# One attention decode kernel: V loads on a second DMA queue, and an output projection in four PSUM banks

## Chip, cores and metric

The kernel runs on one core of one Trainium2 chip. The metric is device time in microseconds for one execution of the whole kernel; each version is given by the median of its runs. The profile is one further look at a single execution, with its own time.

## The reference

One decode step of grouped-query attention with a sliding window, 32 sequences, 32 query heads on 8 key/value heads of 128 elements, bf16. Of the 2048 cached positions only the last W = 512 take part.

```python
B, Sq, D = x.shape                      # 32, 1, 512
Hq, Dh = 32, 128
Hkv, Sk = k_cache.shape[1], k_cache.shape[2]     # 8, 2048
W = min(4096, max(256, Sk // 4))        # 512
rep = Hq // Hkv                         # 4
q = (x @ wq).reshape(B, Sq, Hq, Dh)     # heads moved ahead
k = repeat(k_cache[:, :, Sk - W:, :], rep)
v = repeat(v_cache[:, :, Sk - W:, :], rep)
p = softmax(einsum("bhqd,bhkd->bhqk", q, k) * Dh ** -0.5)
o = einsum("bhqk,bhkd->bhqd", p, v)
return o.reshape(B, Sq, Hq * Dh) @ wo   # (32, 1, 512)
```

Each sequence needs 1 MiB of K and 1 MiB of V. With wq and wo (4 MiB each) that is 72 MiB read from HBM for an output of 32 KB.

## The kernel before

The five engines run their own programs, joined by semaphores. A "batch" is one sequence; its K (and its V) comes as two loads of 512 KB, one per half of the key/value heads (`h` = 0, 1), each into 128 partitions with 4 KB rows. `K_sb` holds `NK` = 6 batches, `V_sb` holds `NV` = 8.

**SP** issues nearly all loads on one DMA queue, in the order of its program: wq in four parts (part 0 at L110, ahead of the block, parts 1 to 3 at L122), then for each `b` `load_k(b)` (L128) and, from `b` = `LEAD` = 5 on, `load_v(b - 5)` (L136). So V follows K at a distance of five batches in the same queue, and after `load_k(31)` come `load_v(26)` to `load_v(31)`. `load_k(b)` waits until PE has transposed batch `b - 6`, `load_v(b)` until PE has done the PV product of batch `b - 8`. Then SP loads wo (L148) into the SBUF space of wq, in four parts cut at heads 0, 10, 20, 28 and 32 (`WO_CUT`), and at the end stores the output (L153). The load of x is issued by ACT ahead of the block (L109).

**PE** computes q transposed (L207) and then runs a loop over `it`. Iteration `it` transposes K of batch `it` (L229, four groups of eight), makes the scores of batch `it - 1` (L246; eight matmuls of 512 columns, four of them beside each other in column groups of 32), and the PV product of batch `it - 6` (L279). The scores of four batches (a "quad") fill one tile `S_ps`, so the softmax runs once per quad; its probabilities are transposed by PE in iterations with `it % 4 == 1` (L261). After the last batch comes the output projection: for each of the 32 heads, four matmuls with 128 columns of wo each, in the four column groups (L301). All 128 add up in one bank, so that the four groups hold four column ranges of the finished output, and `pe_fin` tells that they are done.

**DVE** copies three of the four K^T groups from PSUM (L324), takes the maxima of a quad (L330, L332), scales the probabilities into `P_ex` (L346), copies the PV result into `oT_sb` (L353) and at the end the output (L368).

**ACT** loads its exp table, copies half of q (L375), and then per iteration copies the fourth K^T group (`kt_evac`, L383), per quad computes the exp (`do_exp`, L391) and copies the transposed probabilities (`pt_evac`, L401).

**POOL** makes the constants (`ident`, `perm`, zeros) and copies q into the block layout `QBD` (L189).

The order of instructions within an engine is the order in its program. An engine that waits for a semaphore holds everything behind that wait.

Of the kernel before, what the change touches and what calls it, by code (L numbers as in the profile page):

```python
# [5 lines left out]
BF16 = mybir.dt.bfloat16  # L6
F32 = mybir.dt.float32
ACTF = mybir.ActivationFunctionType
ALU = mybir.AluOpType
# [3 lines left out]
def bass_standalone__sliding_block_cached__sampling_kernel(  # L13
# [8 lines left out]
    B, Sq, D = x.shape  # L22
    _, HKV, SK, DH = k_cache.shape
    HD = wq.shape[1]
    HQ = HD // DH
# [7 lines left out]
    DKT = D // 128  # L33
    SCALE = float(DH) ** -0.5
    P = 128

    NK = 6
    NV = 8
    NKT = 3
    NQB = 8  # L40
    LEAD = 5
    PVLAG = 6
    NQUAD = B // 4
    WO_CUT = (0, 10, 20, 28, 32)

    with ExitStack() as es:
        sb = lambda name, shape, dt: es.enter_context(nc.sbuf_tensor(name, shape, dt))
        ps = lambda name, shape, dt: es.enter_context(nc.psum_tensor(name, shape, dt))
        sem = lambda name: es.enter_context(nc.semaphore(name))

        w_sb = sb("w_sb", [P, DKT * HD], BF16)
        wq_sb = w_sb[:, :].rearrange("p (kt n) -> p kt n", kt=DKT)
        wo_sb = w_sb[:, :].rearrange("p (h n) -> p h n", h=HQ)
# [9 lines left out]
        xT_sb = sb("xT_sb", [P, DKT, 32], BF16)  # L63
        ident = sb("ident", [P, P], BF16)
        perm = sb("perm", [P, G4, NS], BF16)
        x_sb = sb("x_sb", [32, D], BF16)
        out_sb = sb("out_sb", [P, 128], BF16)
        maxv = sb("maxv", [P, NQUAD], F32)
        negmax = sb("negmax", [P, NQUAD], F32)
        sums = sb("sums", [P, NQUAD], F32)  # L70
# [17 lines left out]
        pe_S = sem("pe_S")  # L88
        pe_PT = sem("pe_PT")
        pe_PV = sem("pe_PV")  # L90
        pe_fin = sem("pe_fin")
        pool_perm = sem("pool_perm")
        pool_ex = sem("pool_ex")
        dve_xT = sem("dve_xT")
# [7 lines left out]
        dve_oT = sem("dve_oT")  # L102
        act_exp = sem("act_exp")
        act_PT = sem("act_PT")
        dve_out = sem("dve_out")
        act_warm = sem("act_warm")
        pool_init = sem("pool_init")
        pool_qbd = sem("pool_qbd")
        nc.scalar.dma_start(x_sb[:, :], x.rearrange("b s d -> b (s d)")).then_inc(sem_x, 16)  # L109
        nc.sync.dma_start(wq_sb[:, 0, :], wq[0:P, :]).then_inc(sem_wq[0], 16)  # L110
        block = es.enter_context(nc.Block())

        def score_row(h, j):
# [2 lines left out]
        def cache_rows(cache, b, h):  # L116
            return cache[b, 4 * h:4 * h + 4, SK - W:, :].rearrange("g (s r) d -> s g (r d)", s=NS)

        @block.sync
        def _(sp):  # L120
            for kt in range(1, DKT):
                sp.dma_start(wq_sb[:, kt, :], wq[kt * P:(kt + 1) * P, :]).then_inc(sem_wq[kt], 16)  # L122

            def load_k(b):
                if b >= NK:
                    sp.wait_ge(pe_T[3], b - NK + 1)
                for h in range(2):
                    sp.dma_start(  # L128
                        K_sb[:, b % NK, h].rearrange("p r d -> p (r d)"), cache_rows(k_cache, b, h)
                    ).then_inc(sem_k[b % NK][h], 16)  # L130

            def load_v(b):
                if b >= NV:
                    sp.wait_ge(pe_PV, b - NV + 1)
                for h in range(2):
                    sp.dma_start(  # L136
                        V_sb[:, b % NV, h].rearrange("p r d -> p (r d)"), cache_rows(v_cache, b, h)
                    ).then_inc(sem_v[b % NV], 16)

            for b in range(B + LEAD):  # L140
                if b < B:
                    load_k(b)
                if b >= LEAD:
                    load_v(b - LEAD)
            sp.wait_ge(pe_qt, 1)
            for c in range(4):
                h0, h1 = WO_CUT[c], WO_CUT[c + 1]
                sp.dma_start(  # L148
                    wo_sb[:, h0:h1, :],
                    wo[h0 * DH:h1 * DH, :].rearrange("(h d) n -> d h n", d=P),  # L150
                ).then_inc(sem_wo[c], 16)
            sp.wait_ge(dve_out, 1)
            sp.dma_start(  # L153
                out.rearrange("b s (c n) -> c (b s) n", c=4), out_sb[:, :]
            ).then_inc(sem_out, 16)
            sp.wait_ge(sem_out, 16)

        @block.gpsimd
        def _(pool):
            pool.memset(ident[:, :], 0.0).then_inc(pool_init, 1)  # L160
            pool.wait_ge(pool_init, 1)
            pool.affine_select(
                out=ident[:, :], in_=ident[:, :], compare_op=ALU.not_equal, fill=1.0,
                base=0, pattern=[[-1, P]], channel_multiplier=1,
            ).then_inc(pool_init, 1)
            pool.memset(perm[:, :, :], 0.0).then_inc(pool_perm, 1)
            pool.wait_ge(pool_perm, 1)
            pool.affine_select(
                out=perm[:, :, :], in_=perm[:, :, :], compare_op=ALU.not_equal, fill=1.0,
                base=0, pattern=[[-1, G4], [-G4, NS]], channel_multiplier=1,  # L170
            ).then_inc(pool_perm, 1)
            pool.memset(junk[:, :], 0.0).then_inc(pool_init, 1)
            pool.memset(QBD[:, :, :, :], 0.0).then_inc(pool_init, 1)
            pool.memset(P_ex[:, :, :, :], 0.0).then_inc(pool_ex, 1)
            pool.wait_ge(pool_init, 4)
            pool.wait_ge(dve_qt, 1)
            pool.wait_ge(act_qt, 1)
            for b in range(B):
                if b >= NQB:
                    pool.wait_ge(pe_S, b - NQB + 1)  # L180
                dst = bass.AP(
                    tensor=QBD, offset=(b % NQB) * G * 32 + score_row(0, b % 4),
                    ap=[[NQB * G * 32, P], [G4 * 32 + 16, 2], [32, G4], [1, REP]],
                )
                src = bass.AP(
                    tensor=QT_sb, offset=b,
                    ap=[[HQ * B, P], [G4 * REP * B, 2], [REP * B, G4], [B, REP]],
                )
                pool.tensor_copy(dst, src).then_inc(pool_qbd, 1)  # L189

        @block.tensor
        def _(pe):
# [102 lines left out]
                    pt_transposes((it - 5) // 4)  # L295
            pe.wait_ge(dve_oT, B)
            for hq in range(HQ):
                if hq in WO_CUT:
                    pe.wait_ge(sem_wo[WO_CUT.index(hq)], 16)
                for c in range(4):  # L300
                    ins = pe.matmul(  # L301
                        KT_ps[:, 0, :].bitcast(F32)[32 * c:32 * (c + 1), 0:128],
                        lhsT=oT_sb[:, :, hq],
                        rhs=wo_sb[:, hq, c * 128:(c + 1) * 128],
                        start=(hq == 0), stop=(hq == HQ - 1), tile_position=(0, 32 * c),
                    )
            ins.then_inc(pe_fin, 1)

        @block.vector
        def _(dve):  # L310
# [54 lines left out]
                if it % 4 == 0 and 4 <= it <= B:  # L365
                    softmax_a((it - 4) // 4)
            dve.wait_ge(pe_fin, 1)
            dve.tensor_copy(out_sb[:, :], KT_ps[:, 0, :].bitcast(F32)[:, 0:128]).then_inc(dve_out, 1)  # L368

        @block.scalar  # L370
        def _(act):
            act.wait_ge(pool_init, 3)
            act.activation(junk[:, 1:2], junk[:, 0:1], ACTF.Exp).then_inc(act_warm, 1)
            act.wait_ge(pe_qt, 1)
            act.activation(  # L375
                QT_sb[:, 16:32, :].rearrange("p h b -> p (h b)"), PT_ps[:, 1, :].bitcast(F32), ACTF.Copy
            ).then_inc(act_qt, 1)

            def kt_evac(b):
                if b >= NKT:  # L380
                    act.wait_ge(pe_S, b - NKT + 1)
                act.wait_ge(pe_T[3], b + 1)
                act.activation(  # L383
                    KT_sb[:, b % NKT, 1, 8:16, :, :], KT_ps[:, 3, :], ACTF.Copy
                ).then_inc(act_T, 1)

            def do_exp(q):
                act.wait_ge(dve_sm, 2 * q + 2)
                if q >= 1:
                    act.wait_ge(dve_P, 4 * q)  # L390
                act.activation(  # L391
                    P_f32[:, :], S_ps[:, :], ACTF.Exp,
                    bias=negmax[:, q:q + 1], scale=SCALE, accum_out=sums[:, q:q + 1],
                ).then_inc(act_exp, 1)

            def pt_evac(q):
                if q >= 2:
                    act.wait_ge(pe_PV, 4 * (q - 2) + 4)
                for i in range(2):
                    act.wait_ge(pe_PT, 2 * q + i + 1)  # L400
                    act.activation(  # L401
                        PT_sb[:, q % 2, 8 * i:8 * i + 8, :].rearrange("p r n -> p (r n)"),
                        PT_ps[:, i, :], ACTF.Copy,
                    ).then_inc(act_PT, 1)

            for it in range(B + 2):
                if it < B:
                    kt_evac(it)
                if it % 4 == 0 and 4 <= it:
                    do_exp((it - 4) // 4)  # L410
                if it % 4 == 1 and 5 <= it:
                    pt_evac((it - 5) // 4)


# [26 lines left out]
```

## Time and profile before

| what | value |
|---|---|
| median of 3 runs | 198.01 us (197.91 to 198.32) |
| the profiled execution | 198.32 us, span 196.5 us, 6073 instructions |
| PE busy | 142.8 us (73%) |
| DVE busy | 99.8 us (51%) |
| ACT busy | 56.5 us (29%) |
| POOL busy | 12.1 us (6%) |
| mean TensorE clock granted | 0.851 of full |
| moved by DMA | 75.95 MB, mean 386 GB/s |

The span goes from the first to the last instruction; the execution's own time is longer by what lies around it, here 1.8 us. Busy time counts neither waiting nor the issue of a DMA. Names such as SPq and ACTq stand for an engine's sequencer while it issues a DMA; the transfer itself is run by 16 DMA engines afterwards. In a list of instructions in order of time each line gives the start, the duration, the engine, the source line, the operation with its output and input tiles, how many instructions are merged, and in brackets the idle time of the engine before it with what ended it. In a table by windows each line gives the stretch, its length, the busy time of PE, PE's weight loads, DVE, ACT and POOL with their counts, the granted clock, the busy share of the DMA engines and GB/s.

### The profile page before, as it was taken

To read this page: it belongs to the slowest core of one execution; us is meant where nothing else is said; L and a number is where in the kernel's file an instruction comes from. 1 tells how busy PE (TensorE), PEld (TensorE's weight loads), DVE (VectorE), ACT (ScalarE), POOL (GpSimd) and SP (SyncE) were. 2 spreads that over 40 slices of the span, in tenths; PEclk is the share of its full clock that TensorE was granted. 3 is DMA by queue.
4 is the path that set the end of the run, shared out by engine and by line. 5 is a ranking of instruction groups with operands and counts; after the bars stand their busy time and mean duration, and the time that the engine had idled before them with its cause. 6 is when DMAs were issued, how large, how long until landed. Compare 5 with 4: busy or idle time off the path is not lost.

```text
span 196.5 us, 6073 instructions
## 1 busy us (share of the span) xinstructions
PE 142.8 (73%) x2692; PEld 116.4 (59%) x2692; DVE 99.8 (51%) x187; ACT 56.5 (29%) x67; POOL 12.1 (6%) x43
## 2 busy tenths in 40 slices
PE   0448994987787797749786979779997599746423
PEld 0337773875575576637665858656975477535322
DVE  0006789645774479424952695457645647541000
ACT  3002434433262145203342325232432052320000
POOL 8102000000000010000000000000000000000000
PEclk9999999699999799985999797996699759955555
DMA  5999999999999999999999999999999999999970
GB/s 205 425 417 409 411 405 409 411 409 405 409 409 405 408 407 409 410 407 410 404 409 408 409 409 404 410 406 409 406 408 408 408 409 403 409 404 350 338 253 16
DMA packets 23374, 75.95 MB, mean 386 GB/s; under 512 B 2325, under 2 KB 6453, under 8 KB 22837
## 3 DMA queue, kind: packets, MB, share of 16 engines
q1 hardware_dynamic: 23300, 75.54, 97.5%
q8 instruction: 21, 0.34, 0.7%
q10 hardware_dynamic: 48, 0.03, 0.2%
q14 instruction: 5, 0.03, 0.0%
HBM read 75.53 MB, written 0.03 MB: 384 GB/s over the span
## 4 chain that ended last, share of the span: by engine, by line
SPq 52%; DMA 37%; PE 7%; issue 2%; DVE 0%
DMA K_sb<-in_k_cache_dram 32%; SPq L136 25%; SPq L128 18%; SPq L148 8%; DMA w_sb<-in_wo_dram 5%; PE KT_ps L229 4%; PE QO_ps L279 1%; PE S_ps L246 1%; SPq L122 1%; PE KT_ps L301 0%; SPq L110 0%; DVE out_sb L368 0%
## 5 line engine op out<-in xcount | busy, mean ns | idle before, releaser
L229 PE MATMUL KT_ps<-perm,K_sb 128*128 128x128 bf16 x1024 | 76.0, 238 | 20.7 <-DMA K_sb<-in_k_cache_dram 20.5
L324 DVE COPY KT_sb<-KT_ps 128x1024 bf16<-128x1024 bf16 x96 | 63.3, 687 | 54.0 <-PE KT_ps L229 53.7
L229 PEld LDWEIGHTS KT_ps<-perm,K_sb 128*128 128x128 bf16 x1024 | 67.5, 108 | 27.1 <-DMA K_sb<-in_k_cache_dram 26.0
L383 ACT ACTIVATE KT_sb<-KT_ps 128x1024 bf16<-128x1024 bf16 x32 | 32.7, 1023 | 81.8 <-PE KT_ps L229 81.8
L279 PEld LDWEIGHTS QO_ps<-PT_sb,V_sb 128*128 128x128 bf16 x1024 | 28.2, 98 | 17.4 <-issue 12.7
L279 PE MATMUL QO_ps<-PT_sb,V_sb 128*128 128x16 bf16 x1024 | 31.1, 171 | 3.7 <-DMA V_sb<-in_v_cache_dram 1.9
L346 DVE TENSOR_SCALAR P_ex<-P_f,recip 32x512 bf16<-32x512 f32 x32 | 25.3, 792 | 1.1
L246 PE MATMUL S_ps<-KT_sb,QBD 128*32 128x512 bf16 x256 | 21.4, 414 | 0.0
L401 ACT ACTIVATE PT_sb<-PT_ps 128x1024 bf16<-128x1024 bf16 x16 | 15.5, 1020 | 20.4 <-PE PT_ps L261 20.4
L261 PE MATMUL PT_ps<-ident,P_ex 128*128 128x128 bf16 x128 | 11.8, 266 | 9.6 <-DVE P_ex L346 9.6
L261 PEld LDWEIGHTS PT_ps<-ident,P_ex 128*128 128x128 bf16 x128 | 10.1, 122 | 10.7 <-DVE P_ex L346 10.7
L189 POOL COPY QBD<-QT_sb 128x32 bf16<-128x32 bf16 x32 | 7.4, 245 | 117.9 <-PE S_ps L246 108.0
L353 DVE CAST oT_sb<-QO_ps 128x32 bf16<-128x32 f32 x32 | 5.9, 183 | 8.9 <-PE QO_ps L279 8.8
L301 PE MATMUL KT_ps<-w_sb,oT_sb 128*32 128x128 bf16 x128 | 4.3, 313 | 6.6 <-DMA w_sb<-in_wo_dram 6.6
L207 PE MATMUL PT_ps<-xT_sb,w_sb 128*128 128x32 bf16 x128 | 4.1, 188 | 6.2 <-DMA w_sb<-in_wq_dram 6.2
L301 PEld LDWEIGHTS KT_ps<-w_sb,oT_sb 128*32 128x32 bf16 x128 | 3.3, 158 | 7.4 <-DMA w_sb<-in_wo_dram 4.7
L207 PEld LDWEIGHTS PT_ps<-xT_sb,w_sb 128*128 128x128 bf16 x128 | 3.7, 104 | 6.6 <-DMA w_sb<-in_wq_dram 4.6
L330 DVE TENSOR_REDUCE maxv<-S_ps 128x1 f32<-128x512 f32 x8 | 5.5, 691 | 4.0 <-PE S_ps L246 4.0
L391 ACT ACTIVATE P_f<-S_ps,negmax 128x512 f32<-128x512 f32 x8 | 5.5, 687 | 5.4 <-DVE negmax L332 5.4
L246 PEld LDWEIGHTS S_ps<-KT_sb,QBD 128*32 128x32 bf16 x256 | 3.9, 96 | 3.7 <-issue 1.0
L316 DVE CAST QT_sb<-PT_ps 128x512 bf16<-128x512 f32 x1 | 0.7, 691 | 10.0 <-PE PT_ps L207 10.0
L368 DVE CAST out_sb<-KT_ps 128x128 bf16<-128x128 f32 x1 | 0.3, 292 | 10.7 <-PE KT_ps L301 10.7
(20 smaller groups left out, 11.9 us busy)
## 6 DMA issues: line engine op xcount, KB each, us to landing
K_sb<-in_k_cache_dram SPq DMA_DIRECT2D x64, 512.0 KB, 15.6
V_sb<-in_v_cache_dram SPq DMA_DIRECT2D x64, 512.0 KB, 15.4
w_sb<-in_wq_dram SPq DMA_DIRECT2D x4, 1024.0 KB, 8.4
w_sb<-in_wo_dram SPq DMA_DIRECT2D x2, 1280.0 KB, 19.3
w_sb<-in_wo_dram SPq DMA_DIRECT2D x1, 1024.0 KB, 12.7
w_sb<-in_wo_dram SPq DMA_DIRECT2D x1, 512.0 KB, 9.9
x_sb<-in_x_dram ACTq DMA_DIRECT2D x1, 32.0 KB, 3.2
out_dram<-out_sb SPq DMA_DIRECT2D x1, 32.0 KB
```

Of the source, the lines that this page charges most:

```text
L128: sp.dma_start(K_sb[:, b % NK, h].rearrange("p r d -> p (r d)"), cache_rows(k_cache, b, h)).then_inc(sem_k[b % NK][h], 16)
L136: sp.dma_start(V_sb[:, b % NV, h].rearrange("p r d -> p (r d)"), cache_rows(v_cache, b, h)).then_inc(sem_v[b % NV], 16)
L148: sp.dma_start(wo_sb[:, h0:h1, :], wo[h0 * DH:h1 * DH, :].rearrange("(h d) n -> d h n", d=P),).then_inc(sem_wo[c], 16)
L207: ins = pe.matmul(PT_ps[:, h // 16, :].bitcast(F32)[:, (h % 16) * 32:(h % 16 + 1) * 32], lhsT=wq_sb[:, kt, h * DH:(h + 1) * DH], rhs=xT_sb ...
L229: ins = pe.matmul(KT_ps[:, t, i * 128:(i + 1) * 128], lhsT=K_sb[:, b % NK, h, 8 * (t % 2) + i, :], rhs=perm[:, :, :], start=True, stop=Tru ...
L246: ins = pe.matmul(S_ps[32 * c:32 * c + 32, :], lhsT=QBD[:, b % NQB, g, :], rhs=KT_sb[:, b % NKT, h, :, c, :], start=(j == 0 and h == 0), s ...
L261: ins = pe.matmul(PT_ps[:, r // 8, (r % 8) * 128:(r % 8 + 1) * 128], lhsT=P_ex[:, r, :, :].rearrange("p s g -> p (s g)"), rhs=ident[:, :], ...
L279: ins = pe.matmul(QO_ps[:, 16 * h:16 * h + 16], lhsT=V_sb[:, b % NV, h, r, :], rhs=PT_sb[:, q % 2, r, :].rearrange("p (c n) -> p c n", c=G ...
L324: dve.tensor_copy(KT_sb[:, b % NKT, t // 2, 8 * (t % 2):8 * (t % 2) + 8, :, :], KT_ps[:, t, :]).then_inc(dve_T, 1)
L346: dve.tensor_scalar(P_ex[rows, :, :, c], P_f32[rows, :].rearrange("p (r s) -> p r s", r=NR), recip[rows, q:q + 1], None, op0=ALU.mult,).th ...
L383: act.activation(KT_sb[:, b % NKT, 1, 8:16, :, :], KT_ps[:, 3, :], ACTF.Copy).then_inc(act_T, 1)
L401: act.activation(PT_sb[:, q % 2, 8 * i:8 * i + 8, :].rearrange("p r n -> p (r n)"), PT_ps[:, i, :], ACTF.Copy,).then_inc(act_PT, 1)
```

## The change

All V loads move from SP to ACT. ACT issues `load_v(0)` ahead of its loop and `load_v(it + 1)` at the top of iteration `it`, before `kt_evac(it)`; the wait for the PV product of eight batches earlier moves along. SP keeps x, wq, K, wo and the output. The load of x is now the first on SP's queue, inside the block, and wq part 0 comes behind it. SP loads wo after a new semaphore `act_v`, which ACT raises in iteration 31, one iteration after it has issued the last V load. wo comes in four parts of eight heads.

The output projection has one matmul of 512 columns per head instead of four of 128. Head `hq` goes to column group `hq % 4` and to bank `hq % 4`, so that four banks hold partial sums over eight heads each. DVE copies two of the partial sums into `X_sb` and ACT two; a further matmul with `R_sb` (four identity blocks of 32 below each other, made by POOL) adds the four; ACT copies the sum to `out_sb`, now 32 rows of 512, and SP stores it.

```diff
-    WO_CUT = (0, 10, 20, 28, 32)
+        X_sb = sb("X_sb", [P, D], BF16)
+        R_sb = sb("R_sb", [P, 32], BF16)
-        out_sb = sb("out_sb", [P, 128], BF16)
+        out_sb = sb("out_sb", [32, D], BF16)
...
-        nc.scalar.dma_start(x_sb[:, :], x.rearrange("b s d -> b (s d)")).then_inc(sem_x, 16)
-        nc.sync.dma_start(wq_sb[:, 0, :], wq[0:P, :]).then_inc(sem_wq[0], 16)
...
         def _(sp):
-            for kt in range(1, DKT):
+            sp.dma_start(x_sb[:, :], x.rearrange("b s d -> b (s d)")).then_inc(sem_x, 16)
+            for kt in range(DKT):
                 sp.dma_start(wq_sb[:, kt, :], wq[kt * P:(kt + 1) * P, :]).then_inc(sem_wq[kt], 16)
...
-            for b in range(B + LEAD):
-                if b < B:
-                    load_k(b)
-                if b >= LEAD:
-                    load_v(b - LEAD)
+            for b in range(B):
+                load_k(b)
             sp.wait_ge(pe_qt, 1)
+            sp.wait_ge(act_v, 1)
             for c in range(4):
-                h0, h1 = WO_CUT[c], WO_CUT[c + 1]
                 sp.dma_start(
-                    wo_sb[:, h0:h1, :],
-                    wo[h0 * DH:h1 * DH, :].rearrange("(h d) n -> d h n", d=P),
+                    wo_sb[:, c * 8:(c + 1) * 8, :],
+                    wo[c * 1024:(c + 1) * 1024, :].rearrange("(h d) n -> d h n", d=P),
                 ).then_inc(sem_wo[c], 16)
-            sp.wait_ge(dve_out, 1)
-            sp.dma_start(
-                out.rearrange("b s (c n) -> c (b s) n", c=4), out_sb[:, :]
-            ).then_inc(sem_out, 16)
+            sp.wait_ge(act_out, 1)
+            sp.dma_start(out.rearrange("b s d -> b (s d)"), out_sb[:, :]).then_inc(sem_out, 16)
...
         def _(pool):
...
+            pool.wait_ge(pool_init, 2)
+            pool.tensor_tensor(R_sb[:, :], ident[:, 0:32], ident[:, 32:64], ALU.add).then_inc(pool_R, 1)
...
         def _(pe):
...
             for hq in range(HQ):
-                if hq in WO_CUT:
-                    pe.wait_ge(sem_wo[WO_CUT.index(hq)], 16)
-                for c in range(4):
-                    ins = pe.matmul(
-                        KT_ps[:, 0, :].bitcast(F32)[32 * c:32 * (c + 1), 0:128],
-                        lhsT=oT_sb[:, :, hq],
-                        rhs=wo_sb[:, hq, c * 128:(c + 1) * 128],
-                        start=(hq == 0), stop=(hq == HQ - 1), tile_position=(0, 32 * c),
-                    )
+                c = hq % 4
+                if hq % 8 == 0:
+                    pe.wait_ge(sem_wo[hq // 8], 16)
+                ins = pe.matmul(
+                    KT_ps[:, c, :].bitcast(F32)[32 * c:32 * (c + 1), :],
+                    lhsT=oT_sb[:, :, hq],
+                    rhs=wo_sb[:, hq, :],
+                    start=(hq < 4), stop=(hq >= HQ - 4), tile_position=(0, 32 * c),
+                )
             ins.then_inc(pe_fin, 1)
+            pe.wait_ge(pool_R, 3)
+            pe.wait_ge(dve_x, 2)
+            pe.wait_ge(act_x, 2)
+            pe.matmul(
+                QO_ps[0:32, :], lhsT=R_sb[:, :], rhs=X_sb[:, :], start=True, stop=True, tile_position=(0, 0),
+            ).then_inc(pe_out, 1)
...
         def _(dve):
...
             dve.wait_ge(pe_fin, 1)
-            dve.tensor_copy(out_sb[:, :], KT_ps[:, 0, :].bitcast(F32)[:, 0:128]).then_inc(dve_out, 1)
+            for c in range(2):
+                dve.tensor_copy(
+                    X_sb[32 * c:32 * (c + 1), :], KT_ps[:, c, :].bitcast(F32)[32 * c:32 * (c + 1), :]
+                ).then_inc(dve_x, 1)
...
         def _(act):
...
+            def load_v(b):
+                if b >= NV:
+                    act.wait_ge(pe_PV, b - NV + 1)
+                for h in range(2):
+                    act.dma_start(
+                        V_sb[:, b % NV, h].rearrange("p r d -> p (r d)"), cache_rows(v_cache, b, h)
+                    ).then_inc(sem_v[b % NV], 16)
+
+            load_v(0)
             for it in range(B + 2):
+                if it + 1 < B:
+                    load_v(it + 1)
+                if it == B - 1:
+                    act.activation(junk[:, 0:1], junk[:, 1:2], ACTF.Copy).then_inc(act_v, 1)
                 if it < B:
                     kt_evac(it)
...
+            act.wait_ge(pe_fin, 1)
+            for c in range(2, 4):
+                act.activation(
+                    X_sb[32 * c:32 * (c + 1), :], KT_ps[:, c, :].bitcast(F32)[32 * c:32 * (c + 1), :], ACTF.Copy
+                ).then_inc(act_x, 1)
+            act.wait_ge(pe_out, 1)
+            act.activation(out_sb[:, :], QO_ps[0:32, :], ACTF.Copy).then_inc(act_out, 1)
```

## The prediction

> **What bounds the kernel now.** I read the 40 slices of the span first, then the queues, the chain that ended last, and the instructions of the last 32 us in order of time.
>
> ```profile
> DMA  5999999999999999999999999999999999999970
> GB/s 205 425 417 409 411 405 409 411 409 405 409 409 405 408 407 409 410 407 410 404 409 408 409 409 404 410 406 409 406 408 408 408 409 403 409 404 350 338 253 16
> q1 hardware_dynamic: 23300, 75.54, 97.5%
> SPq 52%; DMA 37%; PE 7%; issue 2%; DVE 0%
> ```
>
> The 16 DMA engines are full from the second slice to the last but one, at about 409 GB/s, all from one queue. The chain is queue and DMA: no compute engine bounds the stream. So an edit costs time if it starts the stream later, leaves a hole in it, slows it, or leaves more work behind its end. The end is this, from the last score-key transposes on:
>
> ```profile
> 165.94 0.90 PEld L229 LDWEIGHTS KT_ps<-perm,K_sb 128*128 128x128 bf16 x16 [0.38 <-DMA K_sb<-in_k_cache_dram]
> ...
> 181.72 1.00 PE L279 MATMUL QO_ps<-PT_sb,V_sb 128*128 128x16 bf16 x32 [0.67 <-DMA V_sb<-in_v_cache_dram]
> 182.76 0.19 DVE L353 CAST oT_sb<-QO_ps 128x32 bf16<-128x32 f32 x1 [1.48 <-PE QO_ps L279]
> ...
> 192.95 0.65 PE L301 MATMUL KT_ps<-w_sb,oT_sb 128*32 128x128 bf16 x16 [0.25 <-DMA w_sb<-in_wo_dram]
> 193.66 0.29 DVE L368 CAST out_sb<-KT_ps 128x128 bf16<-128x128 f32 x1 [10.70 <-PE KT_ps L301]
> 193.97 0.69 SPq L153 DMA_DIRECT2D out_dram<-out_sb  x1
> ```
>
> The second half of K31 lands at 165.94. Six V batches follow it in the one queue (load_k(31) is followed by load_v(26) to load_v(31)); V31 lands at 181.72, so 15.78 us for 6 MiB, **2.63 us per MiB**. The wo weights land 11.23 us later, at 192.95. From K31 to the last oT copy (182.95) the compute chain takes 17.01 us; 0.38 of it is extra waiting for V31 (0.67 against the 0.29 that the matmul group before it waits), so it needs **16.63 us**. Today this chain is hidden: 10 us of wo loads come after it, and three of four projection parts run under them. After the last landing only 0.68 us of matmuls, one copy of 0.29 and the store remain.
>
> **The change, part by part.** *Start.* The queue's first two rows:
>
> ```profile
> 0.74 0.41 SPq L110 DMA_DIRECT2D w_sb<-in_wq_dram  x1
> 1.21 1.83 SPq L122 DMA_DIRECT2D w_sb<-in_wq_dram  x3
> ```
>
> wq part 0 now follows the x load on the same queue. x takes the place at 0.74 (its issue took 0.40 on ACT), wq the one at 1.21: **+0.47 us**, which nothing hides, since the stream is full from there to its end. It is 0 if transfers started later for another reason; I see none.
>
> *V on the ACT queue.* 64 issues leave SP and enter ACT's program, two per batch, before kt_evac. Price of one: 0.61 as for the first K issues with little in flight, 1.08 as for the median of the K row, 3.69 at most in the V row, where SP was held back. I take 1.08, because ACT will issue under load. A batch now lasts 2 x 2.63 = 5.25 us. ACT's own work per batch is 1.02 (copy, L383) + (0.69 + 0.19 + 1.94)/4 = 1.72; with 2.2 of issues 3.9, so ACT keeps up. load_v(b) also waits for PV of batch b-8; queued behind it on ACT are the K^T copy, the exp and the P^T copies, for which PE waits. That PV stands in the PE iteration before the copy's transposes, so the wait ends before PE has made what the copy reads. I cost it at nothing; the cover is 5.25 - 3.9 = 1.3 us per batch. POOL's three adds for R_sb run before 15 us, when POOL is idle: nothing.
>
> *Order of the stream.* This is the large part. Before, V runs five to six batches behind K. Now ACT issues V0 after its QT copy: 14.66 + 0.60 + 0.47 = 15.73. x needed 3.2 us from issue to landing, so V can land from 18.9 on. K's first half batch lands at 14.96 + 0.47 = 15.43, and by 18.9 another 1.33 MiB: K leads by **1.8 batches**. Then both queues have work: six K batches are allowed ahead, and when K(b) lands, V is issued to b+1 and landed to about b-1.8. No row shows two loaded queues; I take equal turns, because the nearest rows, 64 K and 64 V issues of 512 KB, alternate evenly today. The lead then stays. K31 lands when 1.8 V batches are left, not 6: 165.94 + 0.47 + 4.2 x 2.63 = **177.46**. act_v comes one batch earlier, about when K's queue runs out; the V backlog covers the gap. V and wo end as before: 192.95 + 0.47 = 193.42.
>
> *End.* The compute chain gives 177.46 + 16.63 = **194.09** for the last oT copy, now after the last wo part: the chain, not DMA, ends last. All 32 projection matmuls come after it. Nearest rows are the score matmuls, eight of 512 columns in four column groups, two rounds: 0.61 at full clock (the group at 57.35 us), 1.04 at half (68.01). The difference, 0.42, is one half-clock round's worth; so a round is 0.21 or 0.42, plus 0.20 of filling. The clock from 172 us to the end:
>
> ```profile
> 172.00:196.50 24.50, 10.38 (x276) 8.69 (x273) 3.42 (x9) 1.94 (x2) 0.00 (x0) 0.50 0.78 273
> ```
>
> So eight rounds at half clock: 8 x 0.42 + 0.20 = 3.56 (bounds 1.9 at full clock, 4.2 as four score groups). With 0.05 for the handover pe_fin is at **197.70**. Then two DVE copies of 512 columns from PSUM (0.69 each by L316) beside two on ACT (0.60, L375): 1.44 with handover; the summing matmul 0.05 + 0.62; one ACT copy 0.05 + 0.60 + 0.02: 2.78 in all (2.3 to 3.3), against 0.34 now. The store, 32 rows like x, issues in 0.40 for 0.69: 2.24 instead of 2.53 to the span's end. End: 197.70 + 2.78 + 2.24 = 202.72.
>
> **Sum:** +0.47 start, +3.60 from last wo landing to pe_fin (4.28 for 0.68), +2.44 reduction, -0.29 store = **+6.2 us** on the 196.5 us span. The profiled run took 198.32, 0.31 over the median of 198.01; on the median scale 198.01 + 6.2 = **204.2 us**.
>
> The Trainium skill, page "TensorE: Matmul & The Clock Gate", section on the HAM clock gate, says the clock comes up after about 3.4 us of sustained activity; the row above shows 0.50 through 5 us of PV groups, so I stay with half clock, and by the page alone the sum would be near 202.6.
>
> **Rivals.** *The second queue takes other than equal turns, or the projection runs warm.* If ACT's issues come late and K runs further ahead, the projection ends behind the last wo landing: 193.42 + 0.05 + 0.84 + 0.20 = 194.5, end 199.5, time 201.0. If V is served first and no V is left at K31: 177.46 becomes 182.19, time 208.9. For either speaks only that the trace has no row for it. 12% each for 201.0 to 202.5 and 206 to 209.
>
> *ACT becomes the bound.* From a pair of issues above 5.25 - 1.72 = 3.5 us on. The V row holds pairs of 3.44 (0.60 + 2.81), but those fall where one queue carried everything; V alone has some three batches out. At 4.0 per pair: 0.47 x 31 = 14.6 more, 219 us. 6%.
>
> *Faster: two queues lift the stream.* Landings run at 1.049 MB / 2.63 us = 399 GB/s, the engines' mean is 409, wq moved at 425. If two queues even out the engines (2.5% of the 162 us to K31) the time is 200.2; at wq's pace (6.1%) 194.3. It decides from 3.8%, which makes up the 6.2 us. Against it: the 16 engines show 9 of 10 busy throughout and 425 was seen with rows of 8 KB, not 4 KB. 10% that the stream gains over 2%, 7% that the kernel ends faster.
>
> The skill's page "DMA: Bandwidth & Descriptors", section "Rules for kernel authors", says spreading DMAs over issuing engines does not help bandwidth and saves only issue time; no run here shows it yet, and by it this last rival is worth nothing.
>
> **How the numbers follow.** 60% for the forecast, 202.5 to 206.0, at 204.2. The range 200.8 to 209.0 takes in the bounds of the unequal turns on both sides and leaves out ACT as the bound and a stream faster by more than 2.5%. A difference of 0.2% is about what this measurement can tell. Faster 0.07, same 0.02, slower 0.91.
>
> **What would show it.** Right: the first wq issue at about 1.2; DMA full to about 190; the last K transposes near 177.5, the last oT copy near 194 with no wait for wo behind it, 32 projection matmuls in about 3.6, four copies, a matmul and a copy in 2.8. Wrong: K transposes ending far from 177 (turns not equal), PE waiting for ACT's K^T copies in mid-stream (ACT the bound), a GB/s row well off 409, or a projection still waiting for wo.

## The result, and the profile after

The changed kernel takes **203.19 us** (median of 4 runs, 202.91 to 203.54) against 198.02: a ratio of 1.026, with a 95% interval of 1.0238 to 1.0281. It is slower by 5.2 us, where 6.2 were forecast (204.2, range 200.8 to 209.0). The profiled execution, 202.91, is the fastest of the four, where the one profiled before was 0.31 above its median; so the spans lie closer together (196.5 and 201.2, 4.7 apart) than the medians.

The 40 slices, the queues and the chain that ended last, of the changed kernel (span 201.2 us):

```profile
DMA  5999999999999999999999999999999999999800
GB/s 191 417 421 409 408 407 409 411 406 411 406 411 406 412 402 405 411 406 415 402 413 405 408 409 409 409 406 407 412 404 406 411 406 410 388 366 349 292 18 7
q1 hardware_dynamic: 14048, 42.01, 53.6%
q10 hardware_dynamic: 9216, 33.56, 41.9%
DMA 76%; PE 11%; SPq 6%; DVE 3%; ACT 2%; issue 1%; DVEq 0%; ACTq 0%
```

The traffic is split over two queues (q1 is SP's, q10 ACT's), yet the middle of the stream moves at the same 409 GB/s: the second queue brought no bandwidth. What differs is the right-hand edge. Before, the DMA engines were busy until the last slice but one; now two slices of five microseconds have almost no traffic, and PE has 11% of the last chain for 7%. The kernel no longer ends with its transfers.

The end in order of time (columns as in the prediction's list):

```profile
176.59 1.07 PE L227 MATMUL KT_ps<-perm,K_sb 128*128 128x128 bf16 x16 [0.46 <-DMA K_sb<-in_k_cache_dram]
...
193.02 0.19 DVE L357 CAST oT_sb<-QO_ps 128x32 bf16<-128x32 f32 x1 [1.11 <-PE QO_ps L277]
...
193.26 3.15 PE L299 MATMUL KT_ps<-w_sb,oT_sb 128*32 128x512 bf16 x32 [0.28 <-DVE oT_sb L357]
...
196.47 1.20 ACT L436 ACTIVATE X_sb<-KT_ps 32x512 bf16<-32x512 f32 x2 [8.49 <-PE KT_ps L299]
196.47 1.39 DVE L373 CAST X_sb<-KT_ps 32x512 bf16<-32x512 f32 x2 [3.26 <-PE KT_ps L299]
...
197.97 0.38 PE L309 MATMUL QO_ps<-X_sb,R_sb 128*32 128x512 bf16 x1 [1.55 <-DVE X_sb L373]
198.38 0.59 ACT L440 ACTIVATE out_sb<-QO_ps 32x512 bf16<-32x512 f32 x1 [0.70 <-PE QO_ps L309]
198.99 0.36 SPq L147 DMA_DIRECT2D out_dram<-out_sb  x1
```

K31's second half lands at 176.59 instead of 165.94, 10.6 us later. The compute chain from there to the end of the last oT copy (193.21) is as long as ever, 16.62 us. All 32 projection matmuls follow in one piece: the bracket of the 3.15 us group names the oT copy, and no group waits for wo any more. Then come four copies, a matmul and a copy before the store.

### The profile page after: what moved, and what is told of

The parts are those of the page before. It is cut to its first block, busy times and chain, and to the rows that moved or that the text cites. A ratio compares the mean times of both kernels' runs of the same rounds, so it can differ in the third digit from the quotient of the medians.

```text
span 201.2 us, 5894 instructions
## 1 busy us (share of the span) xinstructions
PE 142.7 (71%) x2597; PEld 112.4 (56%) x2597; DVE 101.7 (51%) x188; ACT 58.5 (29%) x71; POOL 13.0 (6%) x46
## 4 chain that ended last, share of the span: by engine, by line
DMA 76%; PE 11%; SPq 6%; DVE 3%; ACT 2%; issue 1%; DVEq 0%; ACTq 0%
DMA K_sb<-in_k_cache_dram 76%; PE KT_ps L227 5%; SPq L133 5%; PE QO_ps L277 3%; PE KT_ps L299 2%; DVE P_ex L350 2%; SPq L127 1%; ACT PT_sb L409 1%; PE S_ps L244 1%; PE PT_ps L259 1%; DVE oT_sb L357 0%; ACT P_f L399 0%; DVEq L45 0%; DVE maxv L334 0%; DVE X_sb L373 0%
## 5 line engine op out<-in xcount | busy, mean ns | idle before, releaser
L227 PE MATMUL KT_ps<-perm,K_sb 128*128 128x128 bf16 x1024 | 77.1, 238 | 33.5 <-DMA K_sb<-in_k_cache_dram 33.0
L328 DVE COPY KT_sb<-KT_ps 128x1024 bf16<-128x1024 bf16 x96 | 64.5, 688 | 61.7 <-PE KT_ps L227 61.3
L277 PEld LDWEIGHTS QO_ps<-PT_sb,V_sb 128*128 128x128 bf16 x1024 | 28.4, 99 | 17.8 <-issue 14.3
L244 PE MATMUL S_ps<-KT_sb,QBD 128*32 128x512 bf16 x256 | 23.5, 451 | 0.0
L259 PE MATMUL PT_ps<-ident,P_ex 128*128 128x128 bf16 x128 | 10.1, 242 | 7.8 <-DVE P_ex L350 7.8
L259 PEld LDWEIGHTS PT_ps<-ident,P_ex 128*128 128x128 bf16 x128 | 8.6, 110 | 8.6 <-DVE P_ex L350 8.6
L383 ACT ACTIVATE QT_sb<-PT_ps 128x512 bf16<-128x512 f32 x1 | 0.6, 598 | 12.3 <-PE PT_ps L205 12.3
L436 ACT ACTIVATE X_sb<-KT_ps 32x512 bf16<-32x512 f32 x2 | 1.2, 590 | 8.5 <-PE KT_ps L299 8.5
L299 PE MATMUL KT_ps<-w_sb,oT_sb 128*32 128x512 bf16 x32 | 3.2, 562 | 0.3 <-DVE oT_sb L357 0.3
## 6 DMA issues: line engine op xcount, KB each, us to landing
V_sb<-in_v_cache_dram ACTq DMA_DIRECT2D x64, 512.0 KB, 16.4
```

What stands on the lines that cost most here:

```text
L227: ins = pe.matmul(KT_ps[:, t, i * 128:(i + 1) * 128], lhsT=K_sb[:, b % NK, h, 8 * (t % 2) + i, :], rhs=perm[:, :, :], start=True, stop=Tru ...
L244: ins = pe.matmul(S_ps[32 * c:32 * c + 32, :], lhsT=QBD[:, b % NQB, g, :], rhs=KT_sb[:, b % NKT, h, :, c, :], start=(j == 0 and h == 0), s ...
L259: ins = pe.matmul(PT_ps[:, r // 8, (r % 8) * 128:(r % 8 + 1) * 128], lhsT=P_ex[:, r, :, :].rearrange("p s g -> p (s g)"), rhs=ident[:, :], ...
L277: ins = pe.matmul(QO_ps[:, 16 * h:16 * h + 16], lhsT=V_sb[:, b % NV, h, r, :], rhs=PT_sb[:, q % 2, r, :].rearrange("p (c n) -> p c n", c=G ...
L299: ins = pe.matmul(KT_ps[:, c, :].bitcast(F32)[32 * c:32 * (c + 1), :], lhsT=oT_sb[:, :, hq], rhs=wo_sb[:, hq, :], start=(hq < 4), stop=(hq ...
L328: dve.tensor_copy(KT_sb[:, b % NKT, t // 2, 8 * (t % 2):8 * (t % 2) + 8, :, :], KT_ps[:, t, :]).then_inc(dve_T, 1)
```

## The experiments

The theory: the loss has two parts. **Order**: V now runs about two batches behind K instead of five to six, so K31 lands later and the chain behind it is no longer hidden by the V and wo loads. **Reduction**: partial sums in four banks need copies, a matmul and a copy behind the projection. The second queue as such costs nothing. The rivals: the projection alone, the second queue alone, or ACT's new issues are the loss.

**e1_proj: the new projection alone.** V and the start are put back to where they were before.

```diff
-            load_v(0)
             for it in range(B + 2):
-                if it + 1 < B:
-                    load_v(it + 1)
...
+            for b in range(B + LEAD):      # on SP, LEAD = 5
+                if b < B:
+                    load_k(b)
+                if b >= LEAD:
+                    load_v(b - LEAD)
```

> V loads back on the sync queue behind K (five batches apart), start as before; only the new projection and its reduction stay. Theory (the later K31 exposes the compute chain, and the projection adds to it only then): K31 lands at 166, the last wo part at 193, only its eight heads (1.1 us for 0.7) and the reduction stage (2.5 for 0.34, store 0.3 shorter) come behind: span 198.8, +2.3, time about 200.3. Rival (the new projection alone is the whole loss): 203.

Measured 200.26 us, ratio to before 1.0106 (1.0089 to 1.0123). Its last lines:

```profile
192.49 1.08 PE L310 MATMUL KT_ps<-w_sb,oT_sb 128*32 128x512 bf16 x8 [1.62 <-DMA w_sb<-in_wo_dram]
193.62 1.20 ACT L434 ACTIVATE X_sb<-KT_ps 32x512 bf16<-32x512 f32 x2 [16.67 <-PE KT_ps L310]
...
196.35 0.37 SPq L158 DMA_DIRECT2D out_dram<-out_sb  x1
```

The last part of wo ends the wait, eight heads follow (1.08 us; before, the last part had four heads and took 0.65), and from their end to the store's issue pass 2.8 us, against 0.4 before. Together with the shorter store and the even parts of wo this is a fixed loss of 2 us; it is not the whole loss. The even parts were not tried by themselves.

**e2_queue: V on ACT with the old projection.** The other half of the change, new start included: four matmuls of 128 columns per head in one bank, one copy.

```diff
-                c = hq % 4
-                ins = pe.matmul(KT_ps[:, c, :]..., rhs=wo_sb[:, hq, :], ...)
+                for c in range(4):
+                    ins = pe.matmul(KT_ps[:, 0, :]..., rhs=wo_sb[:, hq, c * 128:(c + 1) * 128], ...)
```

> V loads on the scalar queue and the start as after; the old projection of 128 matmuls in one bank with its one copy. Theory: last oT copy at 193.2 as in the profile after, then all 128 matmuls (4.3 us at half clock) with no wait for wo, then 0.34 and the store: span 200.4, +3.9, time about 201.9. Rival (the new projection is the whole loss): 198.

Measured 201.61, ratio 1.0174 (1.0151 to 1.0198). K31 lands at 176.37.

**e3_lead1: the order alone, on one queue.** One number of the kernel before is changed.

```diff
-    LEAD = 5
+    LEAD = 1
```

> The kernel before with V one batch behind K instead of five, all on the one sync queue; nothing else. Two V batches are then left when K31 lands. Theory (only the order of the stream counts): K31 at 165.94 + 4 x 2.63 = 176.5, the same end as e2_queue: about 201.8. Rival (a second queue costs by itself, the order does not): 198.0 to 198.5.

Measured 201.76, ratio 1.0174 (1.0134 to 1.0214): the same ratio as e2_queue. This is the run that decides between order and queue, since it has no second queue at all. Its end:

```profile
176.04 1.07 PE L229 MATMUL KT_ps<-perm,K_sb 128*128 128x128 bf16 x16 [0.28 <-DMA K_sb<-in_k_cache_dram]
...
192.47 0.19 DVE L353 CAST oT_sb<-QO_ps 128x32 bf16<-128x32 f32 x1 [1.11 <-PE QO_ps L279]
...
192.71 3.33 PE L301 MATMUL KT_ps<-w_sb,oT_sb 128*32 128x128 bf16 x128 [0.28 <-DVE oT_sb L353]
```

K31 lands at 176.04, the chain takes 16.6 us again (to 192.66), and the projection follows in one piece without waiting for wo. Its 128 small matmuls take 3.33 us, hardly more than the 3.15 of the 32 large ones.

**e4_lead1_proj: one queue, V one batch behind K, new projection.** e1_proj with `LEAD = 1`; the change without its second queue.

> One sync queue with V one batch behind K, and the new projection: the change without its second queue. Theory: as after, 203.0 to 203.3. Rival (the second queue carries part of the loss or gains something): away from 203.2 by that part.

Measured 203.81 (202.66 to 204.60), ratio 1.0276 (1.0236 to 1.0316). Its interval overlaps that of the change, so the second queue is not needed to make the loss. The median is 0.6 above that of the changed kernel, and 0.5 above what was expected; the four runs spread by 1.9 us, and so small a part can't be told from that.

**e5_start: the changed kernel with the old start.**

```diff
-            sp.dma_start(x_sb[:, :], x.rearrange("b s d -> b (s d)")).then_inc(sem_x, 16)
-            for kt in range(DKT):
+            for kt in range(1, DKT):
...
+        nc.scalar.dma_start(x_sb[:, :], x.rearrange("b s d -> b (s d)")).then_inc(sem_x, 16)
+        nc.sync.dma_start(wq_sb[:, 0, :], wq[0:P, :]).then_inc(sem_wq[0], 16)
         block = es.enter_context(nc.Block())
```

> The changed kernel with the old start: x issued by ACT and wq part 0 by SP ahead of the block. Theory from the trace after (wq part 0 landed at 6.18 against 6.22 though issued 0.46 later): no difference, 203.2. Rival (the prediction's own term): 0.47 less, 202.7.

Measured 203.96, but over a spread from 202.49 to 205.15 in six runs: inconclusive for a term of 0.5. The reason for the spread is worth a look (last section).

**e6_late_v: the changed kernel with V issued four iterations later.** Both queues and the whole projection stay; only when ACT issues V is moved (from iteration 28 on it catches up, so that wo is not held back).

```diff
-            load_v(0)
+            nv = 0
             for it in range(B + 2):
-                if it + 1 < B:
-                    load_v(it + 1)
+                upto = it - 2 if it < B - 4 else min(B, 25 + 2 * (it - 27))
+                while nv < upto:
+                    load_v(nv)
+                    nv += 1
```

> The changed kernel, V still on the scalar queue, but ACT issues V of batch it-3 in iteration it instead of it+1 (catching up from iteration 28 on, wo after the last V as in the changed kernel). K then runs some four batches ahead. Theory: K31 lands near 171, the chain ends near 188, under the wo loads; the end is as in e1_proj, about 200.3. Rival (two queues or ACT's issues cost time whatever the order): stays at 203.

Measured 200.79, ratio 1.013 (1.0117 to 1.0143): 2.4 us are back with V still on ACT. K ran further ahead than expected: by the landing of K31, (167.25 - 165.94) / 2.63 = 0.5 of the six batches were lost, so about five and a half were left, not four.

```profile
167.25 1.65 PE L227 MATMUL KT_ps<-perm,K_sb 128*128 128x128 bf16 x16 [1.47 <-DMA K_sb<-in_k_cache_dram]
...
193.03 1.09 PE L299 MATMUL KT_ps<-w_sb,oT_sb 128*32 128x512 bf16 x8 [1.58 <-DMA w_sb<-in_wo_dram]
```

K31 is back at 167.25, and the last projection part waits for wo again. It stays 0.5 above e1_proj.

**e7_late_v_oldproj: two queues, nothing else that costs.** e6_late_v with the old projection and the old start; the semaphore `act_v` ahead of wo stays.

> As e6_late_v, with the old projection and the old start: two queues and nothing else of the change that costs. Theory: 198.0, as before. Rival (the second queue costs or lifts the stream by itself): away from 198.0 by its part; 196 if the queue lifts the stream by 1%.

Measured 198.19 beside 198.22 for the kernel before, ratio 1.0002 (0.9993 to 1.001). A second queue, with 64 issues on ACT, neither costs nor brings anything here as long as K stays well ahead.

**e8_start_only and e9_late_v_oldstart: the start, where it can be measured.** e8 is the kernel before with x first on SP's queue; e9 is e6_late_v with the old start. Both end with their transfers and repeat closely.

> The kernel before with the new start alone: x first on the sync queue inside the block, wq part 0 behind it. Its end is set by the last transfer, so a later stream must show. Prediction's term: +0.47, 198.5. Rival (the start is hidden by something that holds the first transfers anyway, as the landing of wq part 0 at 6.18 against 6.22 suggests): 198.0.

> As e6_late_v (V late on the scalar queue, new projection) with the old start. If the start costs 0.47: 200.3, the same as e1_proj, and e6_late_v's 200.8 is explained. If it costs nothing: 200.8.

e8: 198.30 against 198.15, ratio 1.0009 (1.0 to 1.0018), so between 0 and 0.36 us: below the predicted 0.47. e9: 200.74, the same as e6_late_v's 200.79. By the times, then, the start doesn't explain why those two lie 0.5 above e1_proj. The spans say something else: in the median 199.0 for e6_late_v, 198.6 for e9, 198.5 for e1_proj. The old start takes 0.4 off the span, and the time around the span takes it back: it is 2.1 to 2.3 us in e9 and 1.7 to 1.9 in the other two. In e5_start it is 2.1 to 2.3 too, in e2_queue 1.5, though e7, with the old start and V on ACT, has 1.8 to 1.9. Where this comes from stays open, and so does the 0.5.

The medians together, in us:

| | K31 at 165.6 to 167.6 | K31 at 175.8 to 176.6 |
|---|---|---|
| old projection, one queue | 198.02 (before) | 201.76 (e3_lead1) |
| old projection, two queues | 198.19 (e7) | 201.61 (e2_queue) |
| new projection, one queue | 200.26 (e1_proj) | 203.81 (e4_lead1_proj) |
| new projection, two queues | 200.79, 200.74 (e6, e9) | 203.19 (the change) |

The kernel before measured 198.02 to 198.25 from one occasion to another, so two or three tenths in this table mean nothing. From left to right, the order costs 2.4 to 3.7. From the upper half to the lower, the projection with its reduction costs 1.6 to 2.6. From one queue to two nothing systematic happens. No version was found that beats the kernel before.

## Why the prediction was right, and where its terms were off

**The bound** was read rightly: a full stream with a short end, where a change counts by what it leaves behind the last transfer. That the compute chain would come out from under the wo loads was the main step, and it did: e3_lead1 shows it with the order alone. All the terms that were off were too large. Of the 1.52 us in the span, 0.65 is a clock that rose in the projection of this execution, which does not happen in each, as e4_lead1_proj shows below.

**The compute chain**: 16.63 predicted, 176.59 to 193.21 = 16.62 measured.

**K31's landing**: 177.46 predicted, 176.59 measured. 0.47 of the difference is the start term. The other 0.40 is the lead: (176.59 - 165.94) / 2.63 = 4.05 batches have moved ahead of K31, so 1.95 of 6 are left, not 1.8. The 1.8 had a wrong input: V0 was issued at 14.73, not at 15.73, because ACT's issue did not wait for its copy. With that, and K's first half batch at 14.95 as measured, the prediction's own working gives a lead of 1.6 and, without the start term, 177.5 again: two errors cancel, which is luck. The 0.9 from there to the measured landing was not tried. Part of it may be chance, since e2_queue and e5_start, with V issued in the same places, have K31 at 176.37 and 176.96.

Equal turns were an assumption. They show early in the changed kernel's stream, where both queues have loads waiting (eight V loads had been issued before 25 us, and by the stream's pace three had landed):

```profile
25.45 1.07 PE L227 MATMUL KT_ps<-perm,K_sb 128*128 128x128 bf16 x16 [1.43 <-DMA K_sb<-in_k_cache_dram]
28.00 1.07 PE L227 MATMUL KT_ps<-perm,K_sb 128*128 128x128 bf16 x16 [0.94 <-DMA K_sb<-in_k_cache_dram]
30.55 1.07 PE L227 MATMUL KT_ps<-perm,K_sb 128*128 128x128 bf16 x16 [1.49 <-DMA K_sb<-in_k_cache_dram]
33.11 1.07 PE L227 MATMUL KT_ps<-perm,K_sb 128*128 128x128 bf16 x16 [0.95 <-DMA K_sb<-in_k_cache_dram]
```

Half a batch of K lands every 2.55 us, where the whole stream lands one in 1.31: K has half. Later the program itself keeps K and V at one pace, since ACT issues one V batch per iteration. The times from issue to landing fit:

```profile
K_sb<-in_k_cache_dram SPq DMA_DIRECT2D x64, 512.0 KB, 27.0
V_sb<-in_v_cache_dram ACTq DMA_DIRECT2D x64, 512.0 KB, 16.4
```

K loads took 15.6 us before, in the one queue that they shared with V, and take 27.0 now. At half the pace, 5.25 us per MiB, that is 5.1 MiB: nearly the six batches that K is allowed ahead. V's 16.4 is 3.1 batches, as the prediction counted for V's backlog.

**The start**: +0.47 predicted, 0 to 0.36 measured (e8), though 0.4 in the spans of e6_late_v and e9. The issue did move (1.20 for 0.74), but wq part 0 landed at 6.18 against 6.22. That pair alone says little: in the seven profiles with the old start this part lands anywhere from 5.83 to 6.49, in the four with the new one from 6.16 to 6.25. Adding the issue's whole delay to the end was the error.

**ACT's issues**: costing them at nothing was right (e7), with more room than was counted. One issue took 0.62 in the median, not the 1.08 that was taken; and it can run while an activation runs (last section). PE waited for ACT only once, 1.2 us for the last P^T copies, as before. ACT never became the bound.

**The projection**: 3.61 with handover predicted, 3.20 measured (193.21 to 196.41). Eight rounds at half clock were forecast; the clock stood at 0.50 until 195.7 and at 1.00 from 195.8. In e4_lead1_proj it stayed at 0.50 throughout, and the same 32 matmuls took 3.64, close to the 3.56 that were forecast without the handover:

```profile
192.52 3.64 PE L310 MATMUL KT_ps<-w_sb,oT_sb 128*32 128x512 bf16 x32 [0.28 <-DVE oT_sb L368]
```

So the size was right for one of two cases, and nothing here tells beforehand which one comes. The prediction charged this stretch to the new projection's place behind the chain, and so it is: e2_queue and e3_lead1 pay about the same (3.41 and 3.33) with the old matmuls. It is part of the order's price, not of the projection's shape.

**Reduction and store**: 2.78 predicted from pe_fin to the store's issue, 2.58 measured; the summing matmul took 0.38 for the 0.62 taken, at the higher clock (0.58 in e4_lead1_proj at 0.50). The store 2.24 predicted, 2.21 measured.

Together: -0.47 (start), -0.40 (lead), -0.01 (chain), -0.41 (projection), -0.20 (reduction), -0.03 (store) make 202.72 into the 201.2 of the profile. In the medians the gap is 1.0, since this execution is the fastest of its four.

**The rivals.** ACT as the bound and unequal turns in V's favour did not occur. Two queues that lift the stream are excluded for this kernel by e7 to within about 0.1%. The rule of the Trainium skill's page "DMA: Bandwidth & Descriptors", section "Rules for kernel authors", that spreading DMAs over issuing engines does not help bandwidth, agrees with e7's 198.19 against 198.22.

## What to carry to other kernels

Moving part of a stream to a second queue changes no bandwidth here, but it gives up the order that one queue kept. Two loaded queues shared the engines about equally, so V, which had been scheduled to come late, came early, and K, which it overtook, landed later. The order is then set by when each queue's loads are issued: with V issued four iterations later, the two queues cost nothing (198.19 against 198.22). Count what is left in the stream when the last input of the longest compute chain lands; as long as that outlasts the chain, the kernel ends with its transfers, and once it does not, each further batch moved should cost its full time (worked out from the chain, not tried in steps). Matmuls that leave partial sums in several banks bought nothing here, where the old ones were about as fast (3.33 and 3.41 us against 3.15 to 3.64), and the stage that adds the sums is a fixed tail.

## What the runs showed of the hardware that was not expected

**A DMA issue on ACT runs beside ACT's own work.** From the changed kernel, in order of time:

```profile
14.71 0.60 ACT L383 ACTIVATE QT_sb<-PT_ps 128x512 bf16<-128x512 f32 x1 [12.35 <-PE PT_ps L205]
14.73 2.85 ACTq L418 DMA_DIRECT2D V_sb<-in_v_cache_dram  x4
...
19.69 1.02 ACT L391 ACTIVATE KT_sb<-KT_ps 128x1024 bf16<-128x1024 bf16 x1 [4.38 <-PE KT_ps L227]
19.70 1.45 ACTq L418 DMA_DIRECT2D V_sb<-in_v_cache_dram  x2
```

In these rows the V issues start 0.01 to 0.02 us after the activation that stands before them in the program, and run beside it; they follow its start, not its end. Later issues, which also wait for the PV product of eight batches earlier, come at other distances.

**When the chain sets the end, the time follows the granted clock in the chain.** The kernels that end with their transfers repeat within 0.7 us (before 197.89 to 198.56 in 15 runs, e6_late_v 200.70 to 200.80 in 4). Most of those with the chain exposed spread more: e2_queue 201.25 to 202.34, e3_lead1 200.75 to 202.54, e4_lead1_proj 202.66 to 204.60, e5_start 202.49 to 205.15; only the changed kernel's four lie within 0.63. The windows from 176 to 180 us, where the last K batch is worked on, first of the changed kernel, then of e5_start (columns as before; the granted clock stands third from the end):

```profile
176.00:180.00 4.00, 3.54 (x84) 2.43 (x82) 2.37 (x6) 1.02 (x1) 0.00 (x0) 1.00 0.99 371
```

```profile
176.00:180.00 4.00, 3.04 (x35) 2.01 (x36) 1.34 (x3) 1.02 (x1) 0.00 (x0) 0.63 1.00 353
```

In e5_start the clock was at half for a good part of this stretch; its last transposes took 1.83 us for 1.07 and the chain 17.9 us for 16.6:

```profile
176.96 1.83 PE L228 MATMUL KT_ps<-perm,K_sb 128*128 128x128 bf16 x16 [1.35 <-DMA K_sb<-in_k_cache_dram]
```

The other profiles agree: e2_queue's, of its slowest execution, has 0.59 in this stretch, last transposes of 1.61 and a chain of 17.8; those of e3_lead1 and e4_lead1_proj, each of the fastest execution, have 1.00 and 16.6. That the clock also makes the spread among executions of one kernel is likely but not shown, since each kernel has one profile; the clock averaged over a whole execution doesn't order them (e5_start: 0.868 at 202.49, 0.864 at 204.05). And half clock held on even where PE was mostly busy, in the changed kernel from 188 to 192 us:

```profile
188.00:192.00 4.00, 3.10 (x97) 2.84 (x98) 0.57 (x3) 0.00 (x0) 0.00 (x0) 0.50 0.65 216
```

PE was busy for 3.10 of the 4 us, with gaps of about 0.3 between the PV groups, at a clock of 0.50; it rose only in the projection, which runs without gaps, some 2.5 us after its start. A stretch without gaps is not enough, though: e4_lead1_proj's projection ran 3.64 us without a gap and stayed at 0.50.
